# Token-set steps begun at sooner units, and a DMA scratch of 2,048 bytes, in a one-core FNet plus ReGLU kernel

## The chip, the core and the metric

The kernel runs on one core of a Trainium2 chip. The metric is device time in microseconds (us) of one execution: 1039.16 us is the median of three runs before the change (1038.08, 1039.16 and 1039.48). Five engines work side by side, each through its own instructions in order: TensorE (PE in the profile, its weight loads PEld), VectorE (DVE), ScalarE (ACT), GpSimd (POOL) and SyncE (SP). POOL and SP issue most of the DMAs here; a DMA that waits for something holds up every later instruction of the engine that issues it.

## The reference

```python
def _A_ref(x, dft_seq_re, dft_seq_im, dft_hid_re, dft_hid_im):
    a = jnp.einsum("bsd,ed->bse", x, dft_hid_re)
    b = jnp.einsum("bsd,ed->bse", x, dft_hid_im)
    y = jnp.einsum("ts,bse->bte", dft_seq_re, a) - jnp.einsum("ts,bse->bte", dft_seq_im, b)
    return y

def _B_ref(x, W_gate, W_up, W_down):
    gate = jnp.einsum("bsd,df->bsf", x, W_gate)
    up = jnp.einsum("bsd,df->bsf", x, W_up)
    gate = gate * (lambda x, dt: x.astype(dt))(gate > 0, gate.dtype)
    h = gate * up
    return jnp.einsum("bsf,fd->bsd", h, W_down)

x = A_x
xn = _layernorm(x, axis=-1)
return x + _A_ref(xn, ...) + _B_ref(xn, B_W_gate, B_W_up, B_W_down)
```

S is 2048 tokens, D is 640 and F is 1728, all in float32.

## The kernel before

**Precision and tiling.** Every float32 operand is split in two: ACT writes its rounded high half (line 125) and DVE the rest, the low half (line 126). Each product is three matmuls, high by high, high by low and low by high (lines 131, 132 and 133, the helper `mm3`), with 512 columns. The block products are arranged in Strassen's way, in seven products named B11, T1, B21, T2, B22, T3 and T4.

**Phases.** The sequence phase multiplies the sequence DFT with the normalised tokens, for four chunks of 512 output tokens (c = 0 to 3). The gate and up projections follow, and then the projections back. This change is in the sequence phase.

**Units.** The phase is a list `todo` of units, written by `phase(c, names)`. From T1 on a chunk has 20 units in this order: T10 to T13, T20, B220, T21, B221, T22, T23, B222, B223, T30 to T33, T40 to T43 (the last digit is the group of 256 tokens). A unit of T1 or B22 is 18 matmuls, one of T2, T3 or T4 is 12. Before a unit's matmuls its operand is split into a tile `cb` out of a ring of three buffers: a `cb` can be written once the unit three places ahead of it has been multiplied. The operand comes from SP loads into `raw` and `tk` tiles, which DVE adds up (line 558) and to which POOL adds more from memory with accumulating DMAs (line 694).

**Token sets.** The gate and up projections also need the normalised tokens transposed, as nine sums of blocks (B11 to B22, T1 to T4 and X4), each 128 by 1024. For half of the tokens they are made in the sequence phase and kept in memory as `set1`, in six steps (0 to 5) of `token_sets`. A step takes two `stage` tiles `st`: `mr` for the rows of mean and root, and `ab` for a part of x transposed. The pool has two such buffers in all. A step of 2 to 5 does this:

- POOL loads `mr` (two DMAs at line 426, a row spread over the partitions) and `ab` (two DMAs at line 427);
- DVE makes the normalised blocks in `ab` (lines 432 and 433, twice, 512 columns) and then the four sums T1 to T4 in `mr` (line 439, four times, 256 columns), which replace the rows;
- POOL keeps `ab` and then `mr` (two DMAs at line 448, 512 KB each).

Steps 0 and 1 are shorter (lines 409, 410, 413, 414 and 416, for X4). A step's loads, its making and its keeping are put into the list at the unit where it is begun, and 6 and 8 units later. A step's `mr` and `ab` reuse the buffers of the step before it, so their loads wait until that step's keeps have landed in memory.

**Use of the sets.** In the last chunk the first two sets (T2, then T1) are loaded by SP into `stage` tiles (line 757) and split by ACT and DVE into a tile `r`; five more follow in the same way, through the same two buffers.

**What sets the order.** `SET_UNITS` gives the length of the list at which each step is begun. The order on each engine is then settled when the kernel is built, by a scheduler that places the instructions of the list by its own estimate of when their inputs are there; from then on each engine goes through its instructions in that fixed order. The sums of the tokens (`sums_3`, called V in the list, lines 499 to 501) use `stage` tiles too.

Of the kernel before, what the change touches and what calls it, by code (L numbers as in the profile page):

```python
# [59 lines left out]
def fnet_reglu_kernel(  # L60
# [15 lines left out]
    nc = tc.nc  # L76
# [704 lines left out]
    early_sets, first_sets = list(SETS_A), list(SETS_B)  # L781
    splits = []

    SET_UNITS = (46, 54, 62, 70, 83, 91)

    def phase(c, names):


        for n in names.split():
# [16 lines left out]
            else:  # L806
                stream(c, n[:-1], int(n[-1]))
            if steps and len(todo) >= SET_UNITS[-len(steps)]:
                token_sets(*steps.pop(0))
# [551 lines left out]
```

## Time and profile before

| | |
|---|---|
| median of 3 runs | 1039.16 us |
| the profiled execution, its own time | 1038.61 us |
| its span | 1036.8 us |
| granted TensorE clock, mean | 0.996 |
| PE busy | 1022.1 us |
| DVE, ACT, POOL busy | 771.4, 448.0, 124.8 us |
| moved by DMA | 236.45 MB, mean 228 GB/s |
| of that by POOL's queue | 86.52 MB |

The span is what the profiler saw from the first instruction to the last; the 1.8 us beside it lie around the span. Rows of a timeline have a start, a duration, the engine, the line, the operation and, in brackets, how long the engine stood idle just before and what ended that. Consecutive matmuls overlap: a row of 0.39 us begins 0.227 us after the one before it, so what counts for PE is the start of a row, not its length. DVE's rows overlap likewise by a little.

### The profile page before, as it was taken

The page shows a single profiled execution, that of the slowest core. Times are in us where ns is not written, and L with a number is a line of the kernel's source. Part 1 is how long each engine was busy: PE and PEld are TensorE (multiplying, and loading weights), DVE is VectorE, ACT ScalarE, POOL GpSimd, SP SyncE. Part 2 cuts the span into 40 slices and gives each one's busy share as a digit, 9 for nine tenths or more (in the row PEclk, how much of TensorE's full clock was granted, in tenths as well). Part 3 has the DMA queues.
Part 4 walks back from the last instruction along what each step waited for, and adds up shares of the span by engine and source line. Part 5 has one row for each costly group of instructions (what it writes and reads, how often), then busy time and mean ns, then how long its engine had stood idle before and what let it go on. Part 6 is the DMA issues. An engine that isn't in the chain of part 4 may idle for free.

```text
span 1036.8 us, 12583 instructions
## 1 busy us (share of the span) xinstructions
PE 1022.1 (99%) x4525; PEld 845.2 (82%) x4525; DVE 771.4 (74%) x1081; ACT 448.0 (43%) x571; POOL 124.8 (12%) x193
## 2 busy tenths in 40 slices
PE   9999999999998999999999999999799999999998
PEld 7888888888886888888888888888688888888887
DVE  7967975776857667777887878775486779786777
ACT  6664453333324343433345444443345334543442
POOL 2000013132220112321110000000000001000000
PEclk9999999999999999999999999999899999999999
DMA  8884759989798785854374666652596747994655
GB/s 336 310 274 171 260 159 191 313 221 309 272 224 306 194 205 167 277 206 148 154 256 143 223 234 221 226 213 102 195 360 226 251 127 232 376 339 149 224 166 162
DMA packets 104542, 236.45 MB, mean 228 GB/s; under 512 B 11936, under 2 KB 55328, under 8 KB 102944
## 3 DMA queue, kind: packets, MB, share of 16 engines
q1 hardware_dynamic: 82288, 148.71, 42.6%
q0 software_dynamic: 21760, 86.52, 27.5%
q8 instruction: 35, 0.57, 0.2%
q10 hardware_dynamic: 432, 0.43, 0.1%
q14 instruction: 27, 0.22, 0.1%
HBM read 179.50 MB, written 55.07 MB: 226 GB/s over the span
## 4 chain that ended last, share of the span: by engine, by line
PE 90%; DMA 4%; issue 4%; POOL 1%; DVE 0%; ACT 0%; SPq 0%; POOLq 0%; DVEq 0%
PE ps L132 29%; PE ps L131 29%; PE ps L133 29%; PE ps L519 3%; DMA set<-st 2%; PE ps L548 1%; PE ps L1245 1%; DMA st<-set 1%; DMA wr<-in_hid 0%; DMA raw<-in_dft 0%; POOL tk L694 0%; POOL pq L659 0%; POOL raw L694 0%; DVE cb L126 0%; POOL set L448 0%
## 5 line engine op out<-in xcount | busy, mean ns | idle before, releaser
L131 PE MATMUL ps<-cb,wt 128*128 128x512 f32 x412 | 161.0, 391 | 5.6 <-ACT wt L125 5.6
L133 PE MATMUL ps<-cb,wt 128*128 128x512 f32 x412 | 160.9, 390 | 0.0
L132 PE MATMUL ps<-cb,wt 128*128 128x512 f32 x412 | 160.7, 390 | 0.0
L125 ACT ACTIVATE cb<-rw 128x1024 fp32r<-128x1024 f32 x83 | 82.0, 987 | 123.0 <-PE ps L133 105.9
L126 DVE TENSOR_TENSOR cb<-rw,cb 128x1024 fp32r<-128x1024 f32 x83 | 94.0, 1133 | 53.3 <-ACT cb L125 53.0
L132 PE MATMUL ps<-xs_early,gw 128*128 128x512 f32 x260 | 101.2, 389 | 0.0
L133 PE MATMUL ps<-xs_early,gw 128*128 128x512 f32 x260 | 101.2, 389 | 0.0
L131 PE MATMUL ps<-xs_early,gw 128*128 128x512 f32 x260 | 101.2, 389 | 0.0
L131 PEld LDWEIGHTS ps<-cb,wt 128*128 128x128 f32 x412 | 78.0, 189 | 21.9 <-ACT wt L125 6.0
L126 DVE TENSOR_TENSOR cb<-raw,cb 128x1024 fp32r<-128x1024 f32 x48 | 58.6, 1224 | 47.1 <-ACT cb L125 46.9
L132 PE MATMUL ps<-cb,xs_late 128*128 128x512 f32 x232 | 90.6, 390 | 2.0 <-DVE cb L126 2.0
L131 PE MATMUL ps<-cb,xs_late 128*128 128x512 f32 x232 | 90.5, 390 | 1.3 <-ACT cb L125 1.3
L133 PEld LDWEIGHTS ps<-cb,wt 128*128 128x128 f32 x412 | 77.8, 189 | 16.4 <-DVE wt L126 0.5
L132 PEld LDWEIGHTS ps<-cb,wt 128*128 128x128 f32 x412 | 77.9, 189 | 16.0
L133 PE MATMUL ps<-cb,xs_late 128*128 128x512 f32 x232 | 90.4, 389 | 0.0
L133 PE MATMUL ps<-cb,xs_early 128*128 128x512 f32 x226 | 88.0, 389 | 0.0
L131 PE MATMUL ps<-cb,xs_early 128*128 128x512 f32 x226 | 88.0, 389 | 0.0
L132 PE MATMUL ps<-cb,xs_early 128*128 128x512 f32 x226 | 88.0, 389 | 0.0
L125 ACT ACTIVATE cb<-tk 128x1024 fp32r<-128x1024 f32 x48 | 50.9, 1061 | 84.3 <-PE ps L133 66.8
L126 DVE TENSOR_TENSOR cb<-tk,cb 128x1024 fp32r<-128x1024 f32 x48 | 58.7, 1222 | 31.8 <-ACT cb L125 31.5
L125 ACT ACTIVATE cb<-raw 128x1024 fp32r<-128x1024 f32 x48 | 50.5, 1058 | 73.3 <-PE ps L133 65.8
L122 ACT ACTIVATE gw<-z 128x1024 fp32r<-128x1024 f32 (+1 forms) x52 | 56.1, 1110 | 42.3 <-PE ps L133 29.4
(200 smaller groups left out, 1970.9 us busy)
## 6 DMA issues: line engine op xcount, KB each, us to landing
raw<-in_dft SPq DMA_DIRECT2D x62, 512.0 KB, 5.8
wt<-wparts SPq DMA_DIRECT2D x70, 256.0 KB, 3.1
z<-in_wgu SPq DMA_DIRECT2D x26, 640.0 KB, 4.3
hd<-ob POOLq DMA_DIRECT2D x26, 512.0 KB, 3.7
wparts<-pw POOLq DMA_DIRECT2D x12, 1024.0 KB, 4.1
rw<-hd SPq DMA_DIRECT2D x24, 512.0 KB, 6.4
tk<-in_dft SPq DMA_DIRECT2D x16, 512.0 KB, 6.2
tk<-in_dft POOLq DMA_DIRECT2D x16, 512.0 KB, 7.7
```

What stands on the lines that cost most here:

```text
L122: return nc.scalar.activation(o, i, AF.Copy)
L125: nc.scalar.activation(hi, src, AF.Copy)
L126: return nc.vector.tensor_tensor(lo, src, hi.bitcast(F32), op=OP.subtract)
L131: nc.tensor.matmul(ps, wh, mh, start=first, stop=False, skip_group_check=more)
L132: nc.tensor.matmul(ps, wh, ml, start=False, stop=False, skip_group_check=more)
L133: nc.tensor.matmul(ps, wl, mh, start=False, stop=last, skip_group_check=more)
L519: nc.tensor.matmul(E[0, key], xn_part(n * SG + j, d)[v == 1], b[:, int(v == 2), j], start=False, stop=n % NH == NH - 1 and (j, v) == (SG - ...
L548: nc.tensor.matmul(E[c, key], xn_part(j, d)[v == 1], b[c][0][:, int(v == 2), j], start=j == 0 and v == 0, stop=False)
L1245: nc.tensor.matmul(B[out], w[:, v, oo : oo + P], b, start=False, stop=u == len(units) - 1 and v == 1, skip_group_check=more)
```

## The change

Two numbers change.

```diff
-    SET_UNITS = (46, 54, 62, 70, 83, 91)
+    SET_UNITS = (40, 45, 60, 65, 80, 85)
...
-    nc = bacc.Bacc("TRN2", target_bir_lowering=False, num_devices=1, dynamic_dma_scratch_size=4096)
+    nc = bacc.Bacc("TRN2", target_bir_lowering=False, num_devices=1, dynamic_dma_scratch_size=2048)
```

The list's length grows by one with each unit. The steps were begun 8 units apart, but for 13 between steps 3 and 4; now they come in pairs, 5 units apart within a pair and 15 between pairs. A step's making is still put 6 units after its beginning and its keeping 8. The scratch is the space per partition in which POOL's DMAs are described to the DMA engines. With this edit alone no instruction stands in another place, so the order below is that of the first edit. No instruction is added or removed and PE's order is the same throughout; DVE's, ACT's, POOL's and SP's change between chunk 0 and the start of chunk 3.

**DVE in chunk 1, around step 3.** `tk_1646` was, and `tk_1643` is, the operand of T20; `raw_1711`, now `raw_1748`, that of B220; `tk_1662` that of T21. `st_1668` and `st_1669` are the tiles `mr` and `ab` of step 3. Before:

```order
L558 TENSOR_TENSOR tk_1662<-raw_1770,tk_1662 128x1024
L439 TENSOR_TENSOR st_1616<-st_1617,st_1616 128x256
L126 TENSOR_TENSOR cb_1767<-tk_1646,cb_1767 128x1024
L126 TENSOR_TENSOR cb_1793<-raw_1711,cb_1793 128x1024
L558 TENSOR_TENSOR tk_1682<-raw_1843,tk_1682 128x1024
L126 TENSOR_TENSOR cb_1822<-tk_1662,cb_1822 128x1024
```

Now:

```order
L558 TENSOR_TENSOR tk_1662<-raw_1778,tk_1662 128x1024
L126 TENSOR_TENSOR cb_1775<-tk_1643,cb_1775 128x1024
L432 TENSOR_TENSOR st_1669<-st_1669,st_1668 128x512
L433 TENSOR_TENSOR st_1669<-st_1669,st_1668 128x512
L432 TENSOR_TENSOR st_1669<-st_1669,st_1668 128x512
L433 TENSOR_TENSOR st_1669<-st_1669,st_1668 128x512
L439 TENSOR_TENSOR st_1668<-st_1669 128x256 x2
L439 TENSOR_TENSOR st_1668<-st_1669,st_1668 128x256
L126 TENSOR_TENSOR cb_1807<-raw_1748,cb_1807 128x1024
L439 TENSOR_TENSOR st_1668<-st_1669,st_1668 128x256
```

Step 3 was made after T23's split; it now stands between the splits of T20 and B220. Step 2, whose keeps step 3's loads wait for, moved on DVE from behind the split of T12 to behind that of T10.

**DVE in chunk 2, around step 5.** `st_2219` and `st_2220` were, and `st_2074` and `st_2075` are, the tiles of step 5. Before, the rows from B220's split to T23's:

```order
L126 TENSOR_TENSOR cb_2244<-raw_2163,cb_2244 128x1024
L558 TENSOR_TENSOR tk_2129<-raw_2289,tk_2129 128x1024
L126 TENSOR_TENSOR cb_2286<-tk_2109,cb_2286 128x1024
L558 TENSOR_TENSOR tk_2137<-raw_2313,tk_2137 128x1024
L126 TENSOR_TENSOR cb_2310<-raw_2247,cb_2310 128x1024
L126 TENSOR_TENSOR cb_2317<-tk_2129,cb_2317 128x1024
L432 TENSOR_TENSOR st_2220<-st_2220,st_2219 128x512
L433 TENSOR_TENSOR st_2220<-st_2220,st_2219 128x512
L432 TENSOR_TENSOR st_2220<-st_2220,st_2219 128x512
L126 TENSOR_TENSOR cb_2342<-tk_2137,cb_2342 128x1024
```

Now, the rows from T12's split to B220's:

```order
L126 TENSOR_TENSOR cb_2171<-tk_2145,cb_2171 128x1024
L432 TENSOR_TENSOR st_2075<-st_2075,st_2074 128x512
L126 TENSOR_TENSOR cb_2206<-tk_2165,cb_2206 128x1024
L433 TENSOR_TENSOR st_2075<-st_2075,st_2074 128x512
L432 TENSOR_TENSOR st_2075<-st_2075,st_2074 128x512
L126 TENSOR_TENSOR cb_2230<-tk_2107,cb_2230 128x1024
L433 TENSOR_TENSOR st_2075<-st_2075,st_2074 128x512
L439 TENSOR_TENSOR st_2074<-st_2075 128x256 x2
L439 TENSOR_TENSOR st_2074<-st_2075,st_2074 128x256
L558 TENSOR_TENSOR tk_2123<-raw_2233,tk_2123 128x1024
L439 TENSOR_TENSOR st_2074<-st_2075,st_2074 128x256
L126 TENSOR_TENSOR cb_2256<-raw_2174,cb_2256 128x1024
```

Step 5 was begun on DVE behind T22's split and now begins between those of T12 and T13, six units sooner. Step 4, for whose keeps its loads wait, now begins on DVE behind T42's split of chunk 1 (before: behind T11's of chunk 2); its `ab` is finished behind T43's split and its `mr` behind T10's. On POOL step 5's keeps stand directly behind the accumulating DMA that follows T20's split (`tk_2107`); before, they stood five accumulating DMAs later, behind the one that follows T23's (`tk_2137`).

**ACT in chunk 2, around the splits of the first two sets** (`r1_2626`). Before, from B223's split on:

```order
L125 ACTIVATE cb_2382<-raw_2313 128x1024
L125 ACTIVATE cb_2398<-raw_2163 128x1024
L125 ACTIVATE r1_2626<-st_2627 128x1024
L125 ACTIVATE cb_2421<-raw_2247 128x1024
L125 ACTIVATE r1_2626<-st_2717 128x1024
L125 ACTIVATE cb_2442<-raw_2289 128x1024
```

Now, from T21's split on:

```order
L125 ACTIVATE cb_2279<-tk_2123 128x1024
L125 ACTIVATE cb_2302<-raw_2233 128x1024
L125 ACTIVATE r1_2626<-st_2627 128x1024
L125 ACTIVATE cb_2327<-tk_2145 128x1024
L125 ACTIVATE r1_2626<-st_2717 128x1024
L125 ACTIVATE cb_2344<-tk_2165 128x1024
```

The sets' splits stood around T31's and now stand around T22's, five units sooner, on DVE as well. On SP the first four set loads now come one after the other, ahead of four `raw` loads; before, two of these `raw` loads stood among them.

## The prediction

> **What bounds the kernel now.** I read the head of the page first, then the view of waits for PE, then PE's rows around the waits that lie in the sequence phase, and the chain that leads to them.
>
> ```profile
> span 1036.8 us, 12583 instructions
> PE 1022.1 (99%) x4525; PEld 845.2 (82%) x4525; DVE 771.4 (74%) x1081; ACT 448.0 (43%) x571; POOL 124.8 (12%) x193
> ...
> PE ps L131 <- ACT wt L125: 5.6, 1, 5.6
> PE ps L132 <- DVE cb L126: 2.0, 2, 1.0
> PE ps L131 <- ACT cb L125: 1.3, 1, 1.3
> ```
>
> PE is busy 1022.1 of 1036.8 us, and its matmuls are the same ones after the change. So only its waits can move the time. The wait of 5.6 us for `wt` stands where the projections back begin and is not touched; it moves along with whatever happens ahead of it. The three waits for `cb` are one event in the sequence phase:
>
> ```profile
> 313.91 0.39 PE L133 MATMUL ps<-cb,xs_late 128*128 128x512 f32 x1
> 315.60 0.49 PE L131 MATMUL ps<-cb,xs_late 128*128 128x512 f32 x1 [1.29 <-ACT cb L125]
> 317.04 0.50 PE L132 MATMUL ps<-cb,xs_late 128*128 128x512 f32 x1 [0.95 <-DVE cb L126]
> 321.11 0.50 PE L132 MATMUL ps<-cb,xs_late 128*128 128x512 f32 x1 [1.05 <-DVE cb L126]
> ...
> 299.16 8.49 DMA set<-st
> 307.92 5.60 DMA st<-set
> 313.54 1.07 ACT r L125
> 315.77 0.05 DVE cb L126
> ```
>
> The first four rows are T30's last matmul in chunk 2, T31's first and second, and T32's second. The last should stand 14 matmuls of 0.227 us behind the first, at 317.1; it stands at 321.1. The event costs **4.0 us**. The chain below it says why: step 5's last keep lands at 307.65, SP's first set load starts at 307.92 and lands at 313.5, and ACT and DVE, which go through their work in order, split that set ahead of T31's operand. From ACT's start on the set (313.54) to the second matmul behind it (317.04) pass 3.5 us.
>
> **The change part by part.** Begun sooner, step 5 is kept sooner, and this event goes: **minus 4.0 us**. What takes its place is read from the order in the section on the change. Three rows there can make DVE, and behind it PE, wait for memory: L432 of step 3 ahead of B220's split, L432 of step 5 ahead of T13's, and the set's split ahead of T22's. In the trace no L432 ever waited; it always ran long after its loads.
>
> *Step 3.* Its loads need step 2's keeps to have landed. Rows for DVE's pace, for the hops between POOL and memory, and for PE:
>
> ```profile
> 197.48 1.22 DVE L558 TENSOR_TENSOR tk<-tk,raw 128x1024 f32<-128x1024 f32 x1 [2.46 <-DMA tk<-in_dft]
> 198.62 1.22 DVE L126 TENSOR_TENSOR cb<-tk,cb 128x1024 fp32r<-128x1024 f32 x1
> ...
> 207.77 0.69 DVE L432 TENSOR_TENSOR st<-st 128x512 f32<-128x512 f32 x1
> 208.37 1.22 DVE L558 TENSOR_TENSOR tk<-raw,tk 128x1024 f32<-128x1024 f32 x1
> ...
> 230.94 0.69 DVE L432 TENSOR_TENSOR st<-st 128x512 f32<-128x512 f32 x1
> ...
> 234.61 1.22 DVE L126 TENSOR_TENSOR cb<-raw,cb 128x1024 fp32r<-128x1024 f32 x1
> ...
> 297.17 1.55 DVE L439 TENSOR_TENSOR st<-st 128x256 f32<-128x256 f32 x4
> ...
> 299.16 0.80 POOL L448 DMA_DIRECT2D set<-st  x1 [0.59 <-DVE st L439]
> ...
> 215.53 0.76 POOL L448 DMA_DIRECT2D set<-st  x1 [1.94 <-DVE st L439]
> 220.15 0.74 POOL L427 DMA_DIRECT2D st<-in_xt  x1 [2.06 <-DMA set<-st]
> ...
> 221.89 0.39 PE L132 MATMUL ps<-cb,gw 128*128 128x512 f32 x1
> ```
>
> A full-width row of DVE takes 1.14 us, one of 512 columns 0.60, one of 256 about 0.33. The first add of chunk 1 starts at 197.48, when its load lands. In the new order step 2's `mr` is done six full-width rows, five of 512 and four of 256 later, at 208.7; POOL issues its keep 0.44 us after that (298.72 to 299.16), at 209.2. From a keep's issue to the load that waits for it took 4.6 us near here (215.53 to 220.15), so step 3's L427 goes out at 213.8 (its rows, L426, wait only for the `ab` keep, some 2 us sooner). How long the load then takes is the open price:
>
> ```profile
> L427 POOL DMA_DIRECT2D st<-in_xt x8: 704/724/750, 191.9 to 283.2; - x8
> DMA to landing us min/median/max: 3.5/5.9/8.3
> ...
> L448 POOL DMA_DIRECT2D set<-st x8: 759/780/1108, 212.8 to 299.2; - x8
> DMA to landing us min/median/max: 3.2/7.3/9.6
> ```
>
> I take 4.7, between the least and the median, since the least is the row nearest in time (220.15). L432 then starts at 218.7 with 0.2 for the signal; DVE has reached it at about 216. From L432 to the end of the next split take 4.9 us (230.94 to 234.61 and 1.22), so B220's low half is there at 223.6. PE's second matmul of B220 stood at 221.89: **plus 1.8 us**. At 3.5 us it is 0.6, at 8.3 it is 5.4. What follows has slack again: T21's split ends three rows of DVE later, PE takes 4.1 us for B220.
>
> *Steps 0 to 2.* They are moved too, on POOL past `pq` stores and accumulating DMAs, and V2 and V3 now wait for `stage` buffers that steps 0 and 1 hold. What they feed, T3 of chunk 0, comes ten units later, so I cost them at nothing. The tightest place is B221 of chunk 0, whose low half, by the same count, comes some 0.6 us ahead of PE behind step 1's rows; late loads there would cost up to 2 us. In chunk 1 step 2's rows leave T12's low half about as little.
>
> *Step 5.* The same again, with the rows near its new place:
>
> ```profile
> 256.74 1.28 DVE L561 TENSOR_TENSOR sa<-sa,ps 128x512 f32<-128x512 f32 x2
> ...
> 272.32 0.76 POOL L448 DMA_DIRECT2D set<-st  x1 [11.12 <-DVE st L439]
> 274.32 0.76 POOL L448 DMA_DIRECT2D set<-st  x1
> 278.27 0.72 POOL L426 DMA_DIRECT2D st<-rows  x1 [3.19 <-DMA set<-st]
> 281.80 0.70 POOL L427 DMA_DIRECT2D st<-in_xt  x1 [1.59 <-DMA set<-st]
> ...
> L427 POOL DMA_DIRECT2D st<-in_xt x1: 704/704/704, 281.8 to 281.8; - x1
> DMA to landing us min/median/max: 4.2/4.2/4.2
> ...
> 280.37 0.39 PE L132 MATMUL ps<-cb,xs_early 128*128 128x512 f32 x1
> ...
> 298.05 0.39 PE L132 MATMUL ps<-cb,xs_early 128*128 128x512 f32 x1
> ```
>
> I count in the times of before, without step 3's wait, which shifts DVE, PE and what hangs on them together. From 256.74 the new order brings step 4's `mr` to its end at 267.5 (four full-width rows, eight of 512 and four of 256), and its keep out at 268.0. Such a keep's hop took 7.5 us here (274.32 to 281.80): L427 goes out at 275.4, lands 4.2 us later, and L432 of step 5 starts at 279.8. T12's split has ended at 275.6, six full-width rows and two of 512 behind 267.5; DVE idles four microseconds. T13's low half, one row of 0.60 and one of 1.23 later, is there at 281.6, where PE's second matmul of T13 stood at 280.37: a wait of 1.3 us. Then DVE needs 7.2 us from L432 to the end of step 5's `mr` (three full-width rows, four of 512, four of 256): 287.0. With 0.44 the last keep goes out at 287.5. It took 8.5 us before and 0.3 more to SP; it follows accumulating DMAs now as then, so I keep that: the set load starts at 296.3, lands 5.6 us later, and ACT splits at 301.9. T22's second matmul follows 3.5 us after, at 305.4, where it stood at 298.05. Both waits together: **plus 7.3 us**. T23 then has its operand as PE gets there, and SP's next loads start no later than before.
>
> A rule that speaks for the change: the Trainium skill's "DMA: Bandwidth & Descriptors", in its section "Anatomy of one DMA — SWDGE (gpsimd) path", fits a DMA's time as 2.0 us and the bytes over 436 GB/s. That would be an estimate of 3.2 us for a keep of 512 KB and 2.6 for a load of 256 KB; by it neither wait comes about, and the sum would be minus 4.0. The trace agrees only with its best keep (3.2); the median of eight is 7.3.
>
> *The scratch.* Halved, it holds half the descriptions. Before, POOL's issue of a keep or load took about 0.7 to 1.1 us, and I see no wait in it that a full scratch would explain. I cost it at nothing; it is a rival below.
>
> The sum: minus 4.0, plus 1.8, plus 7.3, is **plus 5.1 us**. The profiled execution took 1038.6 (its span and 1.8 around it), so 1043.7; from the median of the runs, 1039.16, it is **1044.3 us**.
>
> **The rivals.**
>
> - *The transfers are quick, and the new waits stay away: faster.* With the least landings of the rows (3.2 and 3.5) step 3's L432 starts near 216.5 and step 5's at 275.7, behind T12's split without a wait; the last keep goes out at 283.4, lands at 286.6, and a set load of 3.1 us (the least of four) is there at 290, well before T22 needs ACT at 294.5. All 4.0 us are won: 1035.1 us. For it: the order gives POOL's queue more room after step 5. Against it: medians of 7.3 and 5.9.
> - *The waits only change places: no change.* If step 4's keep hops in 5.9 us, as the other one did (272.32 to 278.27), the load in 3.5, and the last keep lands in 6.9, ACT splits at 298.1 and PE loses 3.6 at T22 and 0.6 at B220, against 4.0 before: 1039.4 us.
> - *POOL waits for room in the smaller scratch: slower still.* The place is step 5's last keep, behind the accumulating DMA of T20; if it must wait for that one to land (7.7 us in the row below, issued 3.3 us ahead), everything behind it is 4.4 us later: 1048.7 us. It would show as idle time of POOL that ends with no semaphore.
>
> ```profile
> tk<-in_dft POOLq DMA_DIRECT2D x16, 512.0 KB, 7.7
> ```
>
> That the steps do not come sooner at all is no rival for the early ones, but holds for steps 3 and 5: begun 5 units after the step ahead, they can't load before its keeps land. That is the forecast's mechanism.
>
> **How the numbers follow.** The forecast 0.58, the quick transfers 0.15, the exchange of waits 0.15, the scratch 0.12. What a measurement of this kernel tells from no change is about 0.2%, 2 us. The forecast and the scratch are slower by more than that; of the exchange I give 0.11 to within 2 us and the rest to both sides. So faster 0.17, same 0.11, slower 0.72. The likeliest case by itself runs from 0.6 + 4.2 - 4.0 above the median (step 3's load at its least, step 5 with the quicker hop and a last keep of 6.9) to 5.4 + 9.0 - 4.0 (step 3's load at its most, step 5's at the median): 1040.0 to 1049.6. The range for 8 in 10 takes in the exchange and part of the scratch, and leaves out most of the quick case: 1038 to 1050 us.
>
> **What would show it.** The event at T31 must be gone, and PE must not wait there. Right: DVE idle at L432 in chunk 1 ahead of B220 and in chunk 2 ahead of T13, each ended by a load of `st`, and ACT idle ahead of `r` near 300 us, ended by `st` from `set`, with PE's waits for `cb` adding up to some 9 us. Wrong: L432 without idle time, the last keep out before 284, `r` split before 295. If DVE waits but PE doesn't, I have misjudged the slack; if POOL idles with nothing to wait for, it is the scratch.

## The result, and the profile after

| | before | after |
|---|---|---|
| median, 12 runs each | 1039.01 us | 1037.95 us |
| lowest to highest | 1038.02 to 1040.18 | 1035.80 to 1039.98 |
| span of the profiled execution | 1036.8 us | 1036.6 us |
| PE busy | 1022.1 us | 1024.4 us |

The ratio is 0.9988, with a 95% interval from 0.9979 to 0.9997: the change wins about 1 us, 0.2% at most, where 1044.3 us had been forecast. The small sum hides two large terms.

First the view of waits for PE, of the changed kernel (time in all, times, longest):

```profile
PE ps L132 <- DVE cb L126: 5.4, 3, 4.0
PE ps L113 <- DVE warm L109: 1.1, 1, 1.1
PE ps L131 <- ACT cb L125: 1.0, 1, 1.0
PE ps L548 <- ACT xs_early L250: 0.6, 1, 0.6
```

The waits for `cb` have grown from 3.3 to 6.4 us. The wait of 5.6 us for `wt`, which the prediction said was "not touched", is no longer in the list. So the sequence phase lost time and the start of the projections back won it.

**The loss.** PE's rows of the changed kernel at B220, at T13 and at T22, with two rows where the pace of T13 changes back:

```profile
222.47 0.50 PE L132 MATMUL ps<-cb,gw 128*128 128x512 f32 x1 [0.49 <-DVE cb L126]
...
280.85 0.39 PE L131 MATMUL ps<-cb,xs_early 128*128 128x512 f32 x1
285.23 0.80 PE L132 MATMUL ps<-cb,xs_early 128*128 128x512 f32 x1 [4.00 <-DVE cb L126]
285.83 0.63 PE L133 MATMUL ps<-cb,xs_early 128*128 128x512 f32 x1
...
290.95 0.48 PE L133 MATMUL ps<-cb,xs_early 128*128 128x512 f32 x1
291.26 0.40 PE L131 MATMUL ps<-cb,xs_early 128*128 128x512 f32 x1
...
306.78 0.51 PE L131 MATMUL ps<-cb,xs_early 128*128 128x512 f32 x1 [1.03 <-ACT cb L125]
308.23 0.79 PE L132 MATMUL ps<-cb,xs_early 128*128 128x512 f32 x1 [0.94 <-DVE cb L126]
...
311.72 0.39 PE L131 MATMUL ps<-cb,xs_early 128*128 128x512 f32 x1
```

The waits stand at the three places that the prediction named, and there is none at T31. What it had not named is the pace behind the waits: from 285.23 to 291.26 are 14 matmuls in 6.03 us, where 14 take 3.18 at 0.227 each, and from 308.23 to 311.72 are 8 in 3.49 us in place of 1.82. That is 4.5 us lost in which PE does not wait, but goes at little more than half its pace. DVE, ACT and SP of the changed kernel show where the waits come from:

```profile
217.52 0.69 DVE L432 TENSOR_TENSOR st<-st 128x512 f32<-128x512 f32 x1 [3.65 <-DMA st<-in_xt]
...
283.35 0.69 DVE L432 TENSOR_TENSOR st<-st 128x512 f32<-128x512 f32 x1 [7.02 <-DMA st<-in_xt]
...
296.50 14.48 SPq L757 DMA_DIRECT2D st<-set  x4
...
304.72 1.06 ACT L125 ACTIVATE r<-st 128x1024 fp32r<-128x1024 f32 x1 [8.70 <-DMA st<-set]
```

DVE stands idle at L432 of steps 3 and 5, and ACT ahead of `r`, each until a load lands, as forecast. The end of the phase can be read from a row far behind: ACT's last L976, which waits only for PE, stood at 734.65 and now stands at 742.38. The new order costs **7.7 us** up to there; 5.1 had been forecast.

**The win.** SP's timeline at the start of the projections back, before and then after (a row with x2 runs from the start of the first load to the end of the second):

```profile
708.54 30.52 SPq L1138 DMA_DIRECT2D rw<-pq  x2
739.11 0.42 SPq L1182 DMA_DIRECT2D wr<-in_hid  x1
```

```profile
715.98 2.66 SPq L1138 DMA_DIRECT2D rw<-pq  x2
724.70 0.38 SPq L1182 DMA_DIRECT2D wr<-in_hid  x1
```

Before, the second load of `rw` is held for 30 us; everything behind it on SP is held with it, among that the weights `wr` out of which ACT makes `wt`. PE's rows of before show what it waited for, and what that cost:

```profile
738.31 0.39 PE L133 MATMUL ps<-gw 128*128 128x512 f32 x1
744.25 0.80 PE L131 MATMUL ps<-cb,wt 128*128 128x512 f32 x1 [5.56 <-ACT wt L125]
744.85 0.63 PE L132 MATMUL ps<-cb,wt 128*128 128x512 f32 x1
...
748.40 0.47 PE L131 MATMUL ps<-cb,wt 128*128 128x512 f32 x1
748.71 0.40 PE L132 MATMUL ps<-cb,wt 128*128 128x512 f32 x1
```

The last matmul that reads the buffer `gw` starts at 738.31, and within a microsecond SP goes on. The buffer is named after the gate and up weights; by then it holds the operands of the first unit of the projections back (`lead_split` in the kernel). Behind the wait, 10 matmuls take 4.46 us in place of 2.27. With the changed kernel PE has no wait there and goes at its full pace. The windows view gives the stretch (span, PE busy and its matmuls, granted clock, DMA share, GB/s), of before and of after:

```profile
730.00:760.00 30.00, 24.44 (x99) 0.89 0.78 277
```

```profile
730.00:760.00 30.00, 30.00 (x134) 1.00 0.66 228
```

35 more matmuls fit into the same 30 us: 35 times 0.227 is 7.9 us, which pays for the 7.7.

**Why SP was held.** The order of the instructions does not tell; the waits that the build gives them do (a semaphore is named after the engine or DMA queue that raises it). The second load and the first of `wr`, in before and then in the changed kernel:

```
L1138 DMA rw_5619<-pq2_88 128x1024 [waits DMAHW5_49,DVE_49,PE_49]
L1182 DMA wr_5621<-in_hid 128x2x384 [waits DMAHW0_49]

L1138 DMA rw_5619<-pq2_88 128x1024 [waits DMAHW5_49,DVE_49]
L1182 DMA wr_5621<-in_hid 128x2x384 [waits DMAHW0_49,PE_49]
```

The load has lost its wait for PE; the load of `wr` has gained one, for matmuls that end sooner, as its start at 724.70 shows. The trace says the same. These are lines of before's view of SP's waits, and then one of the changed kernel's, in which neither of the first two stands:

```profile
SPq L1138 <- DVE gw L126: 25.7, 1, 25.7
SPq L1138 <- PE ps L133: 4.1, 1, 4.1
```

```profile
SPq L1182 <- PE ps L133: 6.0, 1, 6.0
```

So the load waited 25.7 us until DVE had written the last operands into `gw`, and 4.1 more until PE had read them. The addresses that the build gave (bytes within a partition; no profile shows them) say why:

| | second `rw` | the buffer of `gw` on the right | overlap |
|---|---|---|---|
| scratch 4,096 | 166,912 to 171,008 | from 170,496 | 512 |
| scratch 2,048 | 164,864 to 168,960 | from 170,496 | none |

With half the scratch the left-hand tile lies 2,048 bytes lower, and the buffer on the right lies where it lay: tiles on the left are laid out behind the scratch, those on the right from the far end. So the second `rw` no longer overlaps a buffer that PE reads up to the end of the first unit of the projections back. (The expectations below call this load the second load of hid, after the kind of its unit.) That is a reading of rows, not yet a test; the first five experiments are the test.

The Trainium skill, in "SBUF — State Buffer", section "SBUF size: 192, 224, or 256?", counts the scratch of the DMA descriptions as taken from each partition's space, 16 KiB of it. The addresses here agree that it is taken from there; its size here is the number in the kernel.

### The profile page after: what moved, and what is told of

It reads as the page before. It is cut to its first block, busy times and chain, and to the rows that moved or that the text cites. A ratio compares the mean times of both kernels' runs of the same rounds, so it can differ in the third digit from the quotient of the medians.

```text
span 1036.6 us, 12590 instructions
## 1 busy us (share of the span) xinstructions
PE 1024.4 (99%) x4525; PEld 846.7 (82%) x4525; DVE 770.9 (74%) x1081; ACT 447.6 (43%) x571; POOL 125.1 (12%) x193
## 4 chain that ended last, share of the span: by engine, by line
PE 90%; DMA 4%; issue 4%; DVE 1%; POOL 1%; ACT 0%; SPq 0%; POOLq 0%; DVEq 0%; ACTq 0%
PE ps L132 29%; PE ps L133 28%; PE ps L131 28%; PE ps L519 3%; DMA set<-st 1%; PE ps L548 1%; DMA pq<-sa 1%; DMA st<-set 1%; PE ps L1245 1%; DMA st<-in_xt 1%; DVE cb L126 0%; DMA raw<-in_dft 0%; DVE st L432 0%; DVE st L433 0%; POOL st L426 0%
## 5 line engine op out<-in xcount | busy, mean ns | idle before, releaser
L132 PE MATMUL ps<-cb,xs_early 128*128 128x512 f32 x226 | 90.2, 399 | 4.9 <-DVE cb L126 4.9
L131 PE MATMUL ps<-cb,xs_early 128*128 128x512 f32 x226 | 89.5, 396 | 1.0 <-ACT cb L125 1.0
L133 PE MATMUL ps<-cb,xs_early 128*128 128x512 f32 x226 | 89.6, 397 | 0.0
```

Source lines behind the costliest of these rows:

```text
L131: nc.tensor.matmul(ps, wh, mh, start=first, stop=False, skip_group_check=more)
L132: nc.tensor.matmul(ps, wh, ml, start=False, stop=False, skip_group_check=more)
L133: nc.tensor.matmul(ps, wl, mh, start=False, stop=last, skip_group_check=more)
```

## The experiments

The theory: two independent terms. The new units cost some 7.7 us in the sequence phase; the smaller scratch wins as much, by addresses alone. Rivals: the size of the scratch itself changes the pace of POOL's DMAs; or the new units bring the loads forward.

**The units alone, and the scratch alone.**

```diff
-    SET_UNITS = (46, 54, 62, 70, 83, 91)
+    SET_UNITS = (40, 45, 60, 65, 80, 85)
```

> The new table of units alone, scratch 4,096 bytes as before. Address theory (the smaller scratch moves the left-hand tiles down, one load of the projections back then no longer overlaps a buffer that TensorE still reads, and only by this does the wait of 5.6 us go): the sequence phase ends some 7.7 us later, and the wait for wt stays, 5 to 6 us: 1046.5 us (1045 to 1048). Rival, the new units by themselves bring those loads forward: the wait for wt is gone and the time is that of the changed kernel, 1038 us. Rival, scratch size (a smaller scratch is slower or faster for GpSimd's queue): the waits of DVE for st in chunks 1 and 2 differ by microseconds from those of the changed kernel.

```diff
-    ... dynamic_dma_scratch_size=4096)
+    ... dynamic_dma_scratch_size=2048)
```

> The scratch of 2,048 bytes alone, the table as before. Address theory: the sequence phase is as before, with its event at T31; the first loads of the projections back start some 15 us or more sooner, PE does not wait for wt, and its matmuls there run at full speed: 1031 us (1030 to 1033). Rival, the scratch costs or wins nothing, as I had costed it: 1039 us. Rival, it holds GpSimd up: over 1040 us, with idle time of POOL that no semaphore ends.

On one chip, with a before of 1039.97 us: the units alone took 1046.19 us (ratio 1.0060, interval 1.0047 to 1.0073), the scratch alone 1031.50 us (0.9923, 0.9909 to 0.9937). PE's waits of the units alone, then SP's timeline of the scratch alone:

```profile
PE ps L132 <- DVE cb L126: 6.7, 4, 4.1
PE ps L131 <- ACT wt L125: 5.6, 1, 5.6
```

```profile
709.24 2.38 SPq L1138 DMA_DIRECT2D rw<-pq  x2
717.67 0.38 SPq L1182 DMA_DIRECT2D wr<-in_hid  x1
```

The new units carry the loss and leave the wait for `wt` as it was; the scratch carries the win, 8.5 us. The rival by which the units bring the loads forward falls. So does the one by which the scratch's size changes POOL's DMAs: DVE's waits at L432 add up to 11.1 us here and to 10.7 in the changed kernel, where the rival asked for microseconds between them.

**Is it the size of the scratch, or where the tiles lie?** Two kernels part these: one moves the tiles without the scratch, the other halves the scratch and puts the tiles back. `LEDGE` and `EDGE` are the bytes of two tiles that nothing reads, at the left and at the right.

```diff
-LEDGE, EDGE = 416, 480
+LEDGE, EDGE = 128, 192
```

> Scratch 4,096 and table as before; only the two unused edge tiles are smaller (left 128 bytes in place of 416, right 192 in place of 480), so that the second load of hid for the projections back ends at 170,720 and the gate/up weight buffer begins at 170,784. Address theory: all of the win of the smaller scratch, with a scratch that is not smaller: 1031 us, no wait for wt. Scratch-size theory: 1039 us, with the wait.

```diff
-LEDGE, EDGE = 416, 480
+LEDGE, EDGE = 2464, 480
...
+    SET_UNITS = (40, 45, 60, 65, 80, 85)
...
+    ... dynamic_dma_scratch_size=2048)
```

> The changed kernel (scratch 2,048, new units), with the left edge tile 2,048 bytes larger, so that every tile lies where it lay before. Address theory: like the new units with the old scratch, 1046.5 us, with the wait for wt back at 5 to 6 us. Scratch-size theory: like the changed kernel, 1038 us.

The second is plain: 1046.98 us (ratio 1.0068, 1.0055 to 1.0081), with the wait back. These are its rows of PE's waits and of SP:

```profile
PE ps L131 <- ACT wt L125: 5.9, 1, 5.9
```

```profile
715.23 30.82 SPq L1138 DMA_DIRECT2D rw<-pq  x2
```

A scratch of 2,048 bytes with the old addresses wins nothing (1046.98 us, and 1046.19 with 4,096; DVE's waits at L432 are 10.6 us). The first was a miss: 1046.84 us (1.0067, 1.0054 to 1.0081) where either theory had expected 1039 or less. Yet its PE does not wait for `wt`; it was busy for longer, 1037.5 us in place of 1022. Groups of PE by shape, of the scratch alone and then of this kernel (count, busy, mean ns, idle time before):

```profile
L131 PE MATMUL ps<-cb,wt 128*128 128x512 f32 x408 | 158.7, 389 | 0.0
L131 PE MATMUL ps<-xs_early,gw 128*128 128x512 f32 x260 | 101.1, 389 | 0.0
...
L131 PE MATMUL ps<-cb,xs_early 128*128 128x512 f32 x226 | 87.9, 389 | 0.0
```

```profile
L131 PE MATMUL ps<-cb,wt 128*128 128x512 f32 x408 | 158.7, 389 | 0.0
L131 PE MATMUL ps<-xs_early,gw 128*128 128x512 f32 x260 | 102.2, 393 | 0.0
...
L131 PE MATMUL ps<-cb,xs_early 128*128 128x512 f32 x226 | 89.4, 396 | 0.0
```

The matmuls on `xs_early` and `gw` take longer, those on `cb` and `wt` do not. In the windows view, of the scratch alone and then of this kernel, that is 12 matmuls fewer in 100 us:

```profile
100.00:200.00 100.00, 100.00 (x443) 1.00 0.79 221
```

```profile
100.00:200.00 100.00, 100.00 (x431) 1.00 0.75 207
```

By the addresses of the build, all these tiles start at multiples of 512 bytes in before. The edit had moved them by 288 bytes, to starts that are odd multiples of 32. So it was made again with 256, which still takes the overlap away, just:

```diff
-LEDGE, EDGE = 416, 480
+LEDGE, EDGE = 160, 224
```

> As the kernel with the smaller edge tiles, but with left 160 and right 224 bytes, so that all tiles move by 256 bytes in place of 288: the second load of hid ends at 170,752, just where the gate/up buffer begins. The kernel with 288 had no wait for wt, yet each three-pass matmul on a moved tile took longer (432 in place of 443 per 100 us). Address theory with alignment (a move by a multiple of 256 keeps the matmuls' pace): 443 matmuls per 100 us, no wait for wt, 1031.5 us with the scratch of 4,096. Rival, the pace was lost for another reason than the 32 bytes by which those tiles are off a multiple of 64: 1045 us or over again. Rival, only the scratch's size wins: 1039 us.

It took 1031.21 us (before 1039.71; ratio 0.9918, 0.9903 to 0.9933), with a scratch of 4,096 bytes. Its SP row and its window:

```profile
709.31 2.38 SPq L1138 DMA_DIRECT2D rw<-pq  x2
```

```profile
100.00:200.00 100.00, 100.00 (x443) 1.00 0.78 223
```

The whole win of the scratch is there without the scratch, and the pace is back at 443. The overlap in addresses was the cause; the size of the scratch does nothing that these runs can tell.

**Which step carries the loss?**

```diff
-    SET_UNITS = (40, 45, 60, 65, 80, 85)
+    SET_UNITS = (40, 45, 60, 65, 80, 91)
```

(the changed kernel is the base here)

> The changed kernel with step 5 begun at unit 91 as before; steps 0 to 4 at the new units. Theory: step 5 alone carries the cost of the table (7.1 us from T13's wait on, 4.1 at T22), and its later start brings back the event at T31 (4.1): PE does not wait at T13 and T22, and the time is 1030.9 us (1030 to 1032.5). Rival, step 3 or the early steps carry a share: 1033 to 1038 us.

It took 1032.26 us (before 1039.71; ratio 0.9928, 0.9911 to 0.9944). Each against the before of its own set of runs, the scratch alone stands at 8.5 us under, the changed kernel at 1.1, this one at 7.5: of the 7.4 us that the units cost in the changed kernel, step 5 carries 6.4, and the other five steps about 1, which is less than the intervals can tell from nothing. The 6.4 is a net sum: PE waits at T31 again (1.35 and 0.95 us), and no longer at T13 and T22, as expected.

**The set's split in the way.** The event at T31 and the wait at T22 are said to be one thing: ACT and DVE stand, in order, at a set that has not landed, with an operand behind it. If so, holding the set's splits back must remove it from either kernel. The first try held them with the means that the code has for operands:

```diff
-            for i in blocks:
-                split(*set_parts(q, i), t[i])
+            with in_turn():
+                for i in blocks: split(*set_parts(q, i), t[i])
```

> The changed kernel, with the splits of the set blocks held until the third-last split of an operand is done, so that ACT and DVE no longer stand in order behind the set load of step 5. Theory: PE's wait at T22 goes, the one at T13 stays as it is, because it comes from L432 ahead of T13's split and not from the set: 4.1 us less than the changed kernel, 1033.9 us. Rival, T22's delay comes from something else (DVE still behind from T13): 1038 us.

> The table of before, the scratch of 2,048, and the splits of the set blocks held back in the same way. Theory: the event at T31 goes without a step being begun sooner, and the loads of the projections back stay early: 1027.4 us, no wait of PE for cb in chunk 2, none for wt. Rival, the set is then late for the first gate/up matmuls, or the next loads into its buffers are: 1031.5 us or more.

Neither moved: 1038.51 us (before 1039.71; 0.9989, 0.9980 to 0.9999) and 1031.17 us (0.9916, 0.9901 to 0.9931). ACT's rows of the second say why:

```profile
314.01 1.06 ACT L125 ACTIVATE r<-st 128x1024 fp32r<-128x1024 f32 x1 [9.50 <-DMA st<-set]
314.98 1.04 ACT L125 ACTIVATE cb<-raw 128x1024 fp32r<-128x1024 f32 x1
```

`in_turn` moved DVE's half of the split only; ACT's half still stood ahead of the operand and waited 9.5 us. These two were no test. The second try holds ACT's half, behind the eighth-last operand that was recorded:

```diff
-        nc.scalar.activation(hi, src, AF.Copy)
+        highs.append(nc.scalar.activation(hi, src, AF.Copy).ins)
...
-            for i in blocks:
-                split(*set_parts(q, i), t[i])
+            with tc.issue_after(highs[-8]):
+                for i in blocks: split(*set_parts(q, i), t[i])
```

> The changed kernel, with ACT's splits of the set blocks held back behind the eighth-last split in program order; the hold of the runs before was on DVE's splits and left ACT's first set split where it stood, ahead of T22's operand. In this build it stands seven operands later on ACT. Theory: PE's wait at T22 goes, the one at T13 stays, since that comes from L432: 4.1 us less than the changed kernel, 1034 us (1033 to 1035.5). Rival, T22 is late because DVE is still behind from T13: PE waits for cb at T22 as before, 1038 us.

> The table of before, the scratch of 2,048, and the same hold on ACT's splits of the set blocks. Theory: the event at T31 goes without a step being begun sooner, and the loads of the projections back stay early: 1027.4 us (1026.5 to 1029), PE waits for cb nowhere in chunk 2. Rival, the set is then late for the first gate/up matmuls, or the loads behind it are late for want of their buffers: 1031.5 us or more, with a wait of PE after 320 us.

On the changed kernel it gave 1033.97 us (before 1039.32; 0.9942, 0.9924 to 0.9960), on the scratch alone 1026.64 us (0.9880, 0.9864 to 0.9895). PE's waits, of the one and of the other:

```profile
PE ps L132 <- DVE cb L126: 5.2, 2, 4.0
PE ps L113 <- DVE warm L109: 1.1, 1, 1.1
```

```profile
PE ps L113 <- DVE warm L109: 1.1, 1, 1.1
```

The wait at T22 goes and the one at T13 stays, as expected: the first was the set, the second L432. (The other wait in the first line, of 1.23 us, is B220's, which the hold does not touch.) In the last kernel PE waits for nothing after its start, and the set is not late for those who use it. It is the fastest of all, 12.7 us under before.

## Why the prediction was wrong

- **The scratch, "I cost it at nothing".** This is the step that failed. It rested on the order of the instructions, which this edit leaves as it is, and looked for a price in POOL's issues alone. The edit moves addresses, with them a wait of SP, and it is worth 8.5 us (1039.97 to 1031.50). The wait for `wt` was set aside as one that "moves along with whatever happens ahead of it". Asked what ended it, before's view of SP's waits would have shown a load into a fresh buffer that waits 25.7 us for DVE and 4.1 for PE, on account of another tile.
- **Minus 4.0 for the event at T31: right.** It is gone from the changed kernel. Taken away by itself, it is worth 4.2 us with each kernel against the before of its own set of runs (8.5 and 12.7 us under), 4.9 by the medians as they stand (1031.50 to 1026.64).
- **Plus 1.8 for step 3: right in kind, too much.** (Its own rows, 223.6 and 221.89, give 1.7.) L432 waited 3.65 us from 213.87 on, and its load was there at 217.5 in place of 218.7. PE waited 0.49 us. That it came so near was in part luck: the load went out at 210.5 in place of 213.8, and took 7.0 us in place of 4.7.
- **Plus 7.3 for step 5: right in kind, too little.** Idle time was not the miss: 4.00 at T13 (1.3 forecast) and 1.03 and 0.94 at T22 (6.0 forecast of both). The loads for L432 went out sooner than counted, from 273.59 (275.4 forecast), but took 9.7 and 9.8 us to land, where 4.2 had been taken from the one row of its kind; why they were slower is open. With more paid at T13, less was left to pay at T22. SP's set load started as forecast (296.50; 296.3) only because two misses cancel: the last keep went out at 291.0 in place of 287.5 and landed in 5.3 us in place of 8.5. The load then took 8.2 us in place of 5.6. The slow pace behind the waits, 4.5 us, was in no term; with it step 5 cost some 10.5 us.
- **The sum of the units, plus 5.1:** 7.7 by ACT's row L976; 6.2 by the median of the units alone (1039.97 to 1046.19), 7.0 by the kernel with the tiles put back.
- **The rivals.** No rival was what happened. The quick transfers did not come: DVE waited 10.7 us for loads at L432. That POOL waits for room in the smaller scratch falls: with the new units and the tiles in the same places, scratches of 4,096 and 2,048 bytes took 1046.19 and 1046.98 us, with the old units and no overlap 1031.21 and 1031.50. That the waits change places names a time near the measured one, 1039.4, but by two waits in the sequence phase, not by one there and one at the projections back.

## What to carry to other kernels

A number that changes how much of a partition is reserved moves the tiles behind it, here by 2,048 bytes. Compare the waits of the two builds, not only the order of their instructions, and for any load that starts late ask which engine ended its wait and whether that engine has any business with the buffer. Where an engine works in order, an early step is only as good as its loads: put whatever must wait for memory behind the operands that are due, as the hold on ACT's splits does, rather than beginning it sooner.

## What the runs showed of the hardware

**A short wait of PE was often followed by slow matmuls.** After the wait of 4.00 us 14 matmuls went at 0.43 us each, and after 5.56 us 10 went at 0.45. So did 8 after the two waits at T22, of 1.03 and 0.94 us, with one matmul between them. The granted clock goes down with them: 0.89 around T13 of the changed kernel, in the windows view.

```profile
270.00:300.00 30.00, 26.00 (x103) 0.89 0.82 233
300.00:340.00 40.00, 38.03 (x160) 0.96 0.84 237
```

How many are slow varies. Behind the same wait at T13 in the changed kernel with ACT's hold it was 7 (PE's rows, the first slow one and the first two at full pace):

```profile
286.55 0.79 PE L132 MATMUL ps<-cb,xs_early 128*128 128x512 f32 x1 [3.99 <-DVE cb L126]
...
289.67 0.39 PE L133 MATMUL ps<-cb,xs_early 128*128 128x512 f32 x1
289.90 0.40 PE L131 MATMUL ps<-cb,xs_early 128*128 128x512 f32 x1
```

And the event at T31, three waits of 1 to 1.3 us, had none in before (clock 1.00 there). With the scratch alone, in the same order, two waits of 1.45 and 0.95 us were followed by about 8:

```profile
317.06 0.51 PE L132 MATMUL ps<-cb,xs_late 128*128 128x512 f32 x1 [0.95 <-DVE cb L126]
...
318.22 0.63 PE L132 MATMUL ps<-cb,xs_late 128*128 128x512 f32 x1
```

The units alone had none behind waits of 1.23, 0.95 and 0.80 us at T22 and T23 (clock 1.00). So the price of much the same wait differs by some 1.5 us from case to case; what decides it was not tried. The Trainium skill, in "TensorE: Matmul & The Clock Gate", section "HAM oscillation — how this bites in real kernels", puts the limit at idle gaps of about 3.4 us, behind which PE starts at half its clock. The waits of 4.00 and 5.56 us agree; T22 in the changed kernel and T31 with the scratch alone, with no wait over 1.5 us, do not, and the measurement decides.

**PE's pace depended on where its operands lie.** With the tiles at odd multiples of 32 bytes the matmuls on `xs_early` and `gw` came at 431 in 100 us, at multiples of 256 at 443. Those on `cb` and `wt` were moved by as much and lost nothing (389 ns), so the start alone does not say which matmul suffers; what does was not tried, nor any other start.
